# Packing the last 96 rows of an MLP weight for four token chunks into three passes of column tiles

## Chip, cores, metric

One core of a Trainium2 chip runs the whole program. The metric is the device time of one execution in microseconds (us). A kernel is run several times; executions of one kernel mostly agree within 0.3%.

Some words used below. TensorE runs the matmuls and the weight loads ahead of them; VectorE and GpSimd work element by element; ScalarE computes the Gelus and Exps; SyncE issues most of the data transfers (DMAs). PSUM is the memory that matmuls write: one bank holds the 512 f32 columns of one matmul here. A column tile is a matmul that uses 32 of the array's 128 columns, written 128*32 in the views. The chain is the profile's path of work and waits, followed back from the last instruction. A line ends with `[idle before <-releaser]` where the engine stood idle before it.

## The reference, cut to what matters

A normalised input feeds a local dilated attention (branch A) and a token mixer with an MLP (branch B); the output is x + A * silu(B). The change sits in the MLP of branch B:

```python
D, F, S = 512, 1376, 2048
x1 = x + hs                                        # mixer output
h2 = gelu(layernorm(x1) @ w3) @ w4                 # w3: 512 x 1376, w4: 1376 x 512
return x1 + h2
```

1376 is 10 x 128 + 96. So w3 gives ten full tiles of 128 rows and one of 96, for each of four chunks of 512 tokens.

## The kernel before

The program sets out its instructions in a fixed order on every engine. The w3 stage lies between the two halves of the attention: for each chunk c, six steps a, each with two row tiles in one PSUM tile of two banks; the last step holds the 96 rows alone.

```python
def w3_pair(c, a):
    pt = psa("w3_ps")                              # next of three PSUM tiles "s", "t", "o", two banks each
    fts = [ft for ft in (2 * a, 2 * a + 1) if ft < NF]          # NF = 11
    for ft in fts:
        fs = P if ft < NF - 1 else FL              # FL = 96
        for dt in range(ND):                       # ND = 4 contraction tiles of 128
            nc.tensor.matmul(pt[:fs, ft % 2, :], lhsT=w3_sb[:, dt, ft * P : ft * P + fs],
                             rhs=x1nT[c][:, dt, :], start=(dt == 0), stop=(dt == ND - 1))
    if len(fts) == 2:
        nc.scalar.activation(h3(c, 2 * a, 2), pt, AF.Gelu_apprx_tanh)
    else:
        nc.scalar.activation(h3(c, NF - 1, 1)[:FL, 0, :], pt[:FL, 0, :], AF.Gelu_apprx_tanh)
# w4_tile: eleven matmuls a token tile, the last with 96 of 128 contraction rows
# ... the stage:
for c in range(NCH):                               # NCH = 4
    for a in range((NF + 1) // 2):
        w3_pair(c, a)
        if c == 0 and a == 0:
            weighted(*prev)()                      # last attention product of half 0, and its copy from PSUM
            prev = None
            ln3_stats(2)                           # layer-norm statistics of chunk 2
            ln3_norm(2)                            # normalise, store to memory
            normalise_dn(0, 2)
            ln3_turn(2)                            # DMA transpose into x1nT[2]
            # ... the same for chunk 3 ...
        if c == 1 and a == 0:
            load_wo()
            load_w4()
            # ...
```

`scores` of attention half 1, which follows, used the PSUM tiles "s" and "t", and `weighted` used "o".

The softmax here doesn't subtract the row's maximum and nothing guards it: scores larger than these inputs give would overflow.

## Time and profile before

| | before |
|---|---|
| time, median of 5 runs | 206.06 us (206.0 to 206.35) |
| span of the profiled run | 204.1 us |
| TensorE busy | 195.2 us, 96% |
| w3 stage, first w3 matmul to first scores | 87.73 to 126.45, that is 38.72 us |
| spacing of 512-column matmuls in the stage | 0.216 us |

The span is what the profiler saw of one execution, from the first to the last instruction; the time of a run is about 2 us more than its span. "Busy" of TensorE counts overlapping matmuls once and says nothing about how well each fills the array. The lines themselves stand in the prediction.

### The profile page before, as it was taken

How to read it: one execution, taken by the hardware profiler on the slowest of the kernel's cores; microseconds unless marked ns; L12 is line 12 of the kernel's file. 1: busy time of each engine (PE TensorE's matmuls, PEld its weight loads, DVE VectorE, ACT ScalarE, POOL GpSimd, SP SyncE). 2: the span in 40 equal slices, each digit the busy share in tenths (PEclk: the TensorE clock that was granted, in tenths of full speed). 3: DMA queues.
4: the chain of work that ended last, by engine and by line, in shares of the span. 5: the costliest groups of instructions: out<-in, count | busy, mean ns of one | idle time of the engine just before them, and what ended most of it. 6: DMA issues, size and time to landing. Idle time of an engine off the chain costs nothing.

```text
span 204.1 us, 4800 instructions
## 1 busy us (share of the span) xinstructions
PE 195.2 (96%) x1900; PEld 94.9 (47%) x1928; DVE 135.0 (66%) x256; ACT 131.5 (64%) x157; POOL 74.5 (37%) x149
## 2 busy tenths in 40 slices
PE   7899999999999999999999999999999999999990
PEld 2585445444444444444444444444555444444440
DVE  5788897626298988856930101288577968888693
ACT  2366768657988888896556657898788877212130
POOL 5889842100023095964691000003830590700000
PEclk9999999999999999999999999999999999999997
DMA  5992264577900089495798948794220241553312
GB/s 146 356 348 80 87 139 86 85 109 112 275 34 5 14 199 140 75 254 107 181 196 184 295 148 136 109 278 156 36 51 5 56 89 26 116 165 118 117 51 77
DMA packets 33197, 26.74 MB, mean 131 GB/s; under 512 B 14600, under 2 KB 31088, under 8 KB 33176
## 3 DMA queue, kind: packets, MB, share of 16 engines
q1 hardware_dynamic: 30984, 23.22, 44.8%
q0 software_dynamic: 2048, 3.09, 8.9%
q8 instruction: 15, 0.25, 0.5%
q10 hardware_dynamic: 144, 0.13, 0.2%
q14 instruction: 6, 0.05, 0.1%
HBM read 12.40 MB, written 4.98 MB: 85 GB/s over the span
## 4 chain that ended last, share of the span: by engine, by line
PE 71%; DVE 11%; DMA 9%; issue 3%; POOL 3%; ACT 2%; SPq 0%; DVEq 0%; POOLq 0%
PE w_ps L501 19%; PE w_ps L521 10%; PE v_ps L547 8%; PE s_ps L567 7%; PE w_ps L457 6%; PE qk_ps L401 5%; PE w_ps L434 5%; PE o_ps L590 4%; PE qk_ps L419 4%; DMA den_d<-orw 3%; PE wo_ps L683 3%; DMA arena<-rden_d 2%; DVE arena L537 2%; DMA rden_d<-rb 1%; DVE arena L691 1%
## 5 line engine op out<-in xcount | busy, mean ns | idle before, releaser
L572 ACT ACTIVATE arena<-s_ps 128x960 bf16<-128x960 f32 (+1 forms) x68 | 62.7, 975 | 13.7 <-PE s_ps L567 13.7
L521 PE MATMUL w_ps<-arena 128*128 128x512 bf16 (+1 forms) x156 | 38.5, 380 | 0.6 <-issue 0.2
L506 ACT ACTIVATE arena<-w_ps 128x1024 bf16<-128x1024 f32 x20 | 20.5, 1024 | 14.5 <-PE w_ps L501 13.1
L632 POOL DMA_DIRECT2D arena<-orw x48 | 25.0, 528 | 5.8 <-DVE orw L602 5.8
L501 PEld LDWEIGHTS <-arena 128*128 128x128 bf16 (+1 forms) x176 | 17.5, 100 | 20.5 <-issue 0.4
L521 PEld LDWEIGHTS <-arena 128*128 128x128 bf16 (+1 forms) x176 | 16.5, 98 | 19.5
L693 POOL TENSOR_TENSOR arena<-arena 128x512 bf16<-128x512 bf16 x6 | 7.7, 1302 | 44.4 <-DVE arena L691 44.4
L536 ACT ACTIVATE sig<-arena 128x512 bf16<-128x512 bf16 x16 | 10.1, 631 | 21.0 <-DVE arena L527 20.9
L551 DVE CAST v_aug<-v_ps 128x512 bf16<-128x512 f32 x17 | 11.7, 690 | 15.4 <-PE v_ps L547 15.3
L602 DVE CAST orw<-o_ps 128x960 bf16<-128x960 f32 (+1 forms) x17 | 19.7, 1156 | 3.1 <-PE o_ps L590 3.0
L401 PE MATMUL qk_ps<-arena 128*128 128x512 bf16 (+1 forms) x109 | 20.4, 332 | 0.5 <-ACT arena L321 0.3
L501 PE MATMUL w_ps<-arena 128*128 128x512 bf16 (+1 forms) x86 | 19.4, 379 | 0.2
L501 PE MATMUL w_ps<-arena,arena 128*128 128x512 bf16 (+1 forms) x86 | 19.1, 379 | 0.1
L547 PE MATMUL v_ps<-wv_sb,arena 128*128 128x512 bf16 x67 | 17.5, 380 | 0.1
L567 PEld LDWEIGHTS <-arena 32*128 32x128 bf16 x544 | 10.2, 92 | 14.8 <-issue 14.7
L567 PE MATMUL s_ps<-arena 32*128 32x120 bf16 (+1 forms) x544 | 16.1, 213 | 0.1
L527 DVE TENSOR_TENSOR arena<-w_ps,arena 128x512 bf16<-128x512 f32 x16 | 11.0, 686 | 7.9 <-PE w_ps L521 7.9
L273 POOL TENSOR_SCALAR l3r<-l3m 128x1 f32<-128x1 f32 (+1 forms) x10 | 2.4, 238 | 37.6 <-DVE l3m L282 37.6
L457 PE MATMUL w_ps<-arena 128*128 128x512 bf16 x63 | 15.2, 380 | 0.1
L660 DVE TENSOR_TENSOR arena<-arena,orw 128x1440 bf16<-128x1440 bf16 (+1 forms) x2 | 1.6, 783 | 19.8 <-DMA orw<-rden_d 19.8
L434 PE MATMUL w_ps<-arena 128*128 128x512 bf16 x63 | 14.6, 379 | 0.0
L401 PEld LDWEIGHTS <-arena 128*128 128x128 bf16 x112 | 10.6, 98 | 7.9 <-DMA arena<-in_A_wqkv_dram 0.8
(99 smaller groups left out, 273.4 us busy)
## 6 DMA issues: line engine op xcount, KB each, us to landing
x1n_dram<-arena SPq DMA_DIRECT2D x5, 512.0 KB, 3.0
arena<-in_A_x_dram SPq DMA_DIRECT2D x4, 512.0 KB, 6.1
arena<-in_A_x_dram SPq DMA_DIRECT2D x6, 256.0 KB, 6.6
out_dram<-arena SPq DMA_DIRECT2D x6, 256.0 KB, 3.6
arena<-in_B_w_dram SPq DMA_DIRECT2D x1, 1376.0 KB
arena<-in_B_w_dram SPq DMA_DIRECT2D x1, 1280.0 KB
arena<-arena SPq DMA_DIRECT2D x16, 72.0 KB, 2.6
arena<-arena SPq DMA_DIRECT2D x16, 68.0 KB, 4.0
```

Of the source, the lines that this page charges most:

```text
L401: nc.tensor.matmul(pt[:, b, hh * w : (hh + 1) * w], lhsT=wqk_sb[:, dt, nt * P : (nt + 1) * P], rhs=xnT[p][:, dt, k * CH + hh * w : k * CH ...
L434: nc.tensor.matmul(pt[:, b, :], lhsT=w1_sb[:, dt, g * P : (g + 1) * P], rhs=xn2T[c][:, dt, :], start=(dt == 0), stop=(dt == ND - 1),)
L457: nc.tensor.matmul(pt, lhsT=w2_src(p, g, m0), rhs=w2_sb[:, g, :], start=(g == 0), stop=(g == ND - 1))
L501: nc.tensor.matmul(pt[:fs, ft % 2, :], lhsT=w3_sb[:, dt, ft * P : ft * P + fs], rhs=x1nT[c][:, dt, :], start=(dt == 0), stop=(dt == ND - 1),)
L506: nc.scalar.activation(h3(c, 2 * a, 2), pt, AF.Gelu_apprx_tanh)
L521: nc.tensor.matmul(pt, lhsT=h3(c, ft, 1)[:fs, 0, jj * P : (jj + 1) * P], rhs=w4_sb[:fs, ft, :], start=(ft == 0), stop=(ft == NF - 1),)
L547: nc.tensor.matmul(vp[:nk, :], lhsT=xnT[p][:, dt, k0 : k0 + nk], rhs=wv_sb[:, dt, :], start=(dt == 0), stop=(dt == ND - 1),)
L551: nc.vector.tensor_copy(out=va[:nk, :, 0:DH], in_=vp[:nk, :].rearrange("p (h d) -> p h d", d=DH))
L567: nc.tensor.matmul(st[:nk, b, i * nq : (i + 1) * nq], lhsT=kT[e][r : r + 32, dt, k0 : k0 + nk], rhs=qT[e][r : r + 32, dt, q0 : q0 + nq], s ...
L572: nc.scalar.activation(prv[:nk, 2 * h : 2 * h + 2], st[:nk, :, 0 : 4 * nq], AF.Exp, scale=SCALE)
L602: nc.vector.tensor_copy(out=orw[p, r][:, :, :, q0 - ra : q0 - ra + nq], in_=op[:, :, 0 : 4 * nq].rearrange("p j (s q) -> p j s q", q=nq),)
L632: nc.gpsimd.dma_start(out=oT[p][DH * hh : DH * (hh + 1), :, ra : ra + rw], in_=orw[p, r][32 * cg : 32 * cg + DH, jj],)
```

## The change

The intent: 96 rows are three column strips of 32. Four chunks have twelve such strips, and the array has room for four at once, so three passes suffice in place of four poorly filled ones. The strips of a chunk no longer lie in order, so one strip of every chunk is zero and the w4 rows are laid out to match. All four chunks must be ready when the packed part runs; it stands at the start of chunk 3.

```diff
+        nc.sync.dma_start(out=w4_sb[FL:P, NF - 1, :], in_=B_w4[F - 32 : F, :])
+    def load_w4x():                                # the same rows moved by 32, for chunks 2 and 3
+        nc.sync.dma_start(out=w4x_sb[32:P, 0, :], in_=B_w4[(NF - 1) * P : F, :])
+        nc.sync.dma_start(out=w4x_sb[0:32, 0, :], in_=B_w4[(NF - 1) * P : (NF - 1) * P + 32, :])
...
+    def w3_packed():
+        pts = [psa("w3_ps") for _ in range(2)]     # chunk c: tile c // 2, bank c % 2
+        for c in range(NCH):
+            g = 3 - c
+            nc.vector.memset(pts[c // 2][32 * g : 32 * g + 32, c % 2, :], 0.0)
+        for n, jobs in enumerate((
+            ((0, 0), (0, 1), (0, 2), (1, 2)), ((1, 0), (1, 1), (2, 1), (2, 2)), ((2, 0), (3, 0), (3, 1), (3, 2)),
+        )):
+            for dt in range(ND):
+                for g, (c, b) in enumerate(jobs):
+                    f0 = (NF - 1) * P + 32 * b
+                    nc.tensor.matmul(
+                        pts[c // 2][32 * g : 32 * g + 32, c % 2, :], lhsT=w3_sb[:, dt, f0 : f0 + 32],
+                        rhs=x1nT[c][:, dt, :], start=(dt == 0), stop=(dt == ND - 1), tile_position=(0, 32 * g),
+                    )
+            if n == 1:
+                nc.scalar.activation(h3_odd, pts[0], AF.Gelu_apprx_tanh)
+        for c in (2, 3):
+            nc.scalar.activation(h3(c, NF - 1, 1)[:, 0, :], pts[1][:, c % 2, :], AF.Gelu_apprx_tanh)
...
-            st = pst("st"[h], "s_ps")
+            st = pst(("st", "to")[p][h], "s_ps")
-        op = pst("o", "o_ps")
+        op = pst("os"[p], "o_ps")
...
-        for a in range((NF + 1) // 2):
+        if c == 3:
+            w3_packed()
+            load_wo()
+            load_w4x()
+        for a in range(NF // 2):
...
-                weighted(*prev)()
+                out = weighted(*prev)
                 prev = None
-                ln3_stats(2)
+                ln3_stats(2, 0, 2)
+                out()
+                ln3_stats(2, 2, 4)
```

More of the change, by code (lines that the diff above doesn't have):

```diff
@@ L85, in at @@
         ar, o = (arenas[0], int(kb * KB)) if kb < 170 else (arenas[1], int((kb - 176) * KB))
-        return ar[:, o : o + n * m].rearrange("p (n m) -> p n m", n=n)
+        return ar[:, o : o + int(n * m)].rearrange("p (n m) -> p n m", n=n)
     xn = [at(8 * p, M // P, D) for p in range(2)]
@@ L109 @@
     w4_sb = at(121.5, NF, D)
+    w4x_sb = at(191, 1, D)
+    h3_odd = at(60, 2, 49.5 * KB)[:, :, 0:CH]
     wo_sb = at(62, ND, D)
@@ L496, in w3_pair @@
         pt = psa("w3_ps")
-        fts = [ft for ft in (2 * a, 2 * a + 1) if ft < NF]
-        for ft in fts:
-            fs = P if ft < NF - 1 else FL
+        for ft in (2 * a, 2 * a + 1):
             for dt in range(ND):
                 nc.tensor.matmul(
-                    pt[:fs, ft % 2, :], lhsT=w3_sb[:, dt, ft * P : ft * P + fs], rhs=x1nT[c][:, dt, :],
+                    pt[:, ft % 2, :], lhsT=w3_sb[:, dt, ft * P : (ft + 1) * P], rhs=x1nT[c][:, dt, :],
                     start=(dt == 0), stop=(dt == ND - 1),
                 )
-        if len(fts) == 2:
-            nc.scalar.activation(h3(c, 2 * a, 2), pt, AF.Gelu_apprx_tanh)
-        else:
-            nc.scalar.activation(h3(c, NF - 1, 1)[:FL, 0, :], pt[:FL, 0, :], AF.Gelu_apprx_tanh)
+        nc.scalar.activation(h3(c, 2 * a, 2), pt, AF.Gelu_apprx_tanh)
+    def w3_packed():
[17 more added lines that the diff above has]
+            nc.scalar.activation(h3(c, NF - 1, 1)[:, 0, :], pts[1][:, c % 2, :], AF.Gelu_apprx_tanh)
     def w4_tile(t):
@@ L519, in half @@
             for ft in range(lo, hi):
-                fs = P if ft < NF - 1 else FL
+                w = w4_sb[:, ft, :] if ft < NF - 1 or c < 2 else w4x_sb[:, 0, :]
                 nc.tensor.matmul(
-                    pt, lhsT=h3(c, ft, 1)[:fs, 0, jj * P : (jj + 1) * P], rhs=w4_sb[:fs, ft, :],
+                    pt, lhsT=h3(c, ft, 1)[:, 0, jj * P : (jj + 1) * P], rhs=w,
                     start=(ft == 0), stop=(ft == NF - 1),
@@ L881 @@
     for c in range(NCH):
-        for a in range((NF + 1) // 2):
+        if c == 3:
[3 more added lines that the diff above has]
+        for a in range(NF // 2):
+            if c == 3 and a == 1:
+                normalise_end(0, 1)
+                normalise_end(0, 2)
             w3_pair(c, a)
             if c == 0 and a == 0:
-                weighted(*prev)()
+                out = weighted(*prev)
                 prev = None
-                ln3_stats(2)
+                ln3_stats(2, 0, 2)
+                out()
+                ln3_stats(2, 2, 4)
                 ln3_norm(2)
@@ L898 @@
             if c == 1 and a == 0:
-                load_wo()
                 load_w4()
@@ L904 @@
                 spread(1, CUT, M)
-            if c == 2 and a == 0:
-                normalise_end(0, 1)
-                normalise_end(0, 2)
     for k in range(2):
```

## The prediction

> **What bounds the kernel now.** I first read the page: busy shares, slices and the chain that ended last.
>
> ```profile
> PE 195.2 (96%) x1900; PEld 94.9 (47%) x1928; DVE 135.0 (66%) x256; ACT 131.5 (64%) x157; POOL 74.5 (37%) x149
> ...
> PE   7899999999999999999999999999999999999990
> ...
> PE 71%; DVE 11%; DMA 9%; issue 3%; POOL 3%; ACT 2%; SPq 0%; DVEq 0%; POOLq 0%
> ```
>
> TensorE is busy in nearly every slice and holds 71% of the chain, so what the change is worth is the TensorE time that it takes away, unless a wait opens. Second I read the timeline of TensorE over the w3 stage, which is the part that is rewritten.
>
> ```profile
> 87.73 1.89 PE L501 MATMUL w_ps<-arena 128*128 128x512 bf16 x8
> 89.55 0.60 PE L590 MATMUL o_ps<-arena,v_aug 128*32 128x120 bf16 x32
> 90.08 7.94 PE L501 MATMUL w_ps<-arena 128*128 128x512 bf16 x35
> 97.86 19.16 PE L501 MATMUL w_ps<-arena,arena 128*128 128x512 bf16 x86
> 116.85 9.66 PE L501 MATMUL w_ps<-arena 128*128 128x512 bf16 x43
> 126.45 0.71 PE L567 MATMUL s_ps<-arena 32*128 32x128 bf16 x16
> ```
>
> The stage runs from 87.73 to 126.45 without an idle gap. Chunk 0 holds 11 tiles of 4 matmuls. Behind the attention piece (L590), 36 matmuls remain from 90.08 to 97.86: 7.78 / 36 = 0.216 us each (a duration of 379 ns is latency; they overlap). All of chunks 1 to 3 gives 28.59 / 132 = 0.2166, which I call 0.216. Third, I read the groups by shape: does a 96-column tile cost less?
>
> ```profile
> L501 PE MATMUL w_ps<-arena,arena 128*96 128x512 bf16 x8 | 2.1, 379 | 0.0
> L501 PE MATMUL w_ps<-arena 128*96 128x512 bf16 x8 | 2.1, 379 | 0.0
> ```
>
> It does not: 379 ns, as the full ones. The last 96 rows cost 4 chunks x 4 matmuls x 0.216 = 3.45 us, with a quarter of the array empty.
>
> **What a packed pass will cost.** The kernel already has 128x32 column tiles: the attention output L590, four at a time. I looked at L590 in very narrow windows of the timeline; the first column shows when the oldest matmul still in flight had begun.
>
> ```profile
> 89.55 0.24 PE L590 MATMUL o_ps<-arena,v_aug 128*32 128x120 bf16 x4
> 89.61 0.38 PE L590 MATMUL o_ps<-arena,v_aug 128*32 128x120 bf16 x16
> 89.66 0.38 PE L590 MATMUL o_ps<-arena,v_aug 128*32 128x120 bf16 x16
> 89.71 0.38 PE L590 MATMUL o_ps<-arena,v_aug 128*32 128x120 bf16 x16
> 89.77 0.38 PE L590 MATMUL o_ps<-arena,v_aug 128*32 128x120 bf16 x16
> 89.82 0.33 PE L590 MATMUL o_ps<-arena,v_aug 128*32 128x120 bf16 x12
> 89.92 0.23 PE L590 MATMUL o_ps<-arena,v_aug 128*32 128x120 bf16 x4
> ```
>
> Four matmuls start together, and the next four 0.053 us later. At the 512-column rate that 0.216 us gives, 120 columns take 0.051 us: the four cost about what one would, and their weight loads are hidden. The price is at the ends. Chunk 0 from 87.73 to 97.86 takes 10.13 us; 44 x 0.216 = 9.50 and eight groups x 0.053 = 0.42 leave 0.21 us. I take 0.2 us for entering and leaving the tiled mode once.
>
> **What the Trainium skill says.** "TensorEngine Tiling (Array Packing)", Key Properties, says that tiles work in parallel and that changing the tiling mode drains the engine; the trace agrees, with 0.2 us for both ends. "TensorE: Matmul & The Clock Gate", Measured speedup vs the span model, gives a pack of n tiles the duration of one matmul plus about 4 ns per further tile; its 3-tile pack with 512 columns gained 2.38x. The trace of before is kinder in a stream (0.053 us per four), because one pack follows another. "PSUM — Partial Sum Buffer", The four PSUM rules, says that a group's first matmul clears status bits only in the bank and the 32-partition quadrants that it writes. So four groups can be open in four quadrants, and the zeroed quadrant survives. No run so far shows this; a correct result would.
>
> **The change, part by part.**
> (1) Removed: 16 matmuls with 96 columns, 3.45 us, all on the path.
> (2) Added: 3 passes x 4 contraction tiles = 12 groups of four, 12 x 0.216 = 2.59 us, plus one switch of mode, 0.2 us. Sum of (1) and (2): 3.45 - 2.79 = 0.66 us saved.
> (3) w4 keeps 176 matmuls, 16 of them with contraction 128 in place of 96. The groups by shape give 381 against 380 ns: nothing. The extra w4 rows are 32 + 128 rows of 1 KB, small beside the 1280 KB load.
> (4) ScalarE: four 96x512 Gelus of 0.58 us become one of 1.02 and two of 0.58. Nothing on the path, except at the end of the stage, where the last Gelu now has 1024 columns: 0.44 us later, ahead of the Exp table load (1.28) and the first two Exps (1.94).
> (5) Four 32-partition memsets on VectorE, which does little from 105 to 126; I estimate 0.6 us each from the 0.67 to 0.69 us of its other 512-element f32 work. In the built program the first packed weight load waits for those of the first tile, and a later one for those of the second. The first slot's previous Gelu ends some 2 us before the packed part, the second's some 0.5 us before. The second pair ends about 0.8 us after the packed part has begun, and is wanted at about 0.96 us, when the second pass begins. It just fits.
> (6) PSUM names of the last attention phase are rotated by one. The sequence with 24 instead of 27 allocations ends one further round, so this keeps the old distance between users. One gain: the first scores waited for a slot,
>
> ```profile
> 126.51 0.65 PE s_ps L567 x16
> 127.16 3.78 PE w_ps L521 x17
> 130.94 0.35 PE s_ps L567 x16
> ```
>
> 0.65 us where the next sixteen take 0.35. Their second slot is now released by the last but one pair's Gelu, so 0.3 us is won. But the Exps come 0.44 us later relative to TensorE, and the second scores' second half then waits for them about 0.2 us. I count 0.05 us saved net.
> (7) Statistics in two parts. Chunks now take 40 instead of 44 matmuls, so chunk 2 starts at 87.73 + 10.13 - 0.86 + 8.63 = 105.63 instead of 107.4, and chunk 3's data are wanted in the third pass at about 116.0 instead of 116.85. When do the transposed inputs come?
>
> ```profile
> 94.97 1.05 POOL L274 TENSOR_TENSOR l3r<-l3r,nhalf 128x4 f32<-128x4 f32 x1
> ...
> 101.23 2.20 SPq L488 DMA_TRANSPOSE arena<-x1n_dram  x1
> ...
> 108.55 3.21 SPq L488 DMA_TRANSPOSE arena<-x1n_dram  x1
> ```
>
> These transposes land 4.4 to 5.2 us after issue: 105.6 to 106.4 for chunk 2, just too late for 105.63. The split moves two of the four statistics into VectorE's idle time before 90.2 (1.7 us), and two normalisations ahead of the second root on GpSimd (another 0.7). The chain then ends some 2.4 us earlier, chunk 2 lands near 103.5, with 2 us in hand, and chunk 3 near 111. So this part pays nothing by itself; it protects the 0.66.
> (8) The wo load moves behind the sixteen copies of SyncE (121.5 to 132.2 before). w4 goes some 2.5 us earlier without wo and the copies follow, so wo should be issued near 128.5 and land by 135; its first matmul comes at 138.3.
>
> Sum: 0.66 + 0.05 = 0.7 us saved, 206.06 - 0.7 = 205.35 us. After the stage the path is TensorE to 172, then TensorE beside the last normalisation, all timed from TensorE, so the gain should arrive at the end undiminished.
>
> **Rivals.**
> A. The inputs are late: the packed part pulls the demand forward, and transposes and their stores vary with DMA load. If the split does not help, chunk 2 waits up to 0.8 us: 205.35 + 0.8 = 206.15, no gain. Against it are 2 us of margin.
> B. Four streams of 512 columns from four different sources do not run together. Wholly serial they would cost 48 x 0.216 = 10.4 us, so 213.8; partly, with 10% more per group, 0.26 us, so 205.6. L590 speaks against it, with four different moving operands too, but at 120 columns, in one bank.
> C. The wait moves: to memsets or, behind the stage, to the longer last Gelu or a late wo. The first costs up to 0.3 us (205.65), the second up to 0.3, a late wo perhaps 1 to 2 (206.4 to 207.4). For it speaks that (5) and (6) have margins under 0.2 us; against it that wo has 3 us.
>
> **Range and chances.** All the likely terms are tenths: 0.66 plus or minus 0.2 for group and switch, minus 0.3 for C, and run-to-run scatter of 0.15. Low end 204.9 (a switch cheaper and the score gain whole), high end 206.0 (A or two small waits). Two per cent is 4.1 us; nothing here could save it, as the whole removed work is 3.45. Slower by 4.1 needs B in full. Faster 0.01, within 2% 0.98, slower 0.01.
>
> **What would show it.** In the changed profile: packed groups of four spaced 0.216 us, the packed part near 2.8 us, the w3 stage 38.72 - 0.66 = 38.06 us from its first matmul to the first scores, no gap at the starts of chunk 2 and of the third pass, transposes of chunk 2 issued near 98.8, wo landed before its first matmul, the first scores 0.35 us. Group spacing over 0.25 us, a TensorE gap before chunk 2, or an idle TensorE before the wo matmul would make the prediction wrong.

## The result

The changed kernel took 205.22 us (median of 5, 204.95 to 205.27) against 206.06. The ratio is 0.9952, with a 95% interval of 0.9939 to 0.9966. Ratios here are the mean time of one kernel's runs over that of the other's of the same rounds, so not quite the ratio of the medians. Executions over 1.5% slower than the fastest of the same kernel are left out of the means. The forecast was 205.35, in a range of 204.9 to 206.0.

Two lines of the changed kernel's page: busy times, and the chain that ended last by engine.

```profile
PE 193.4 (95%) x1932; PEld 93.7 (46%) x1960; DVE 137.3 (67%) x260; ACT 131.6 (65%) x156; POOL 76.3 (38%) x151
...
PE 83%; DVE 7%; POOL 3%; issue 2%; ACT 2%; DMA 1%; POOLq 0%
```

TensorE sets the time, as before. The 71% of the chain that the prediction quotes is not a mark of the old kernel: a second profile of it has the chain line above word for word, 83%. Now the timeline of TensorE over the stage (start, duration, line, operation, destination and sources, count):

```profile
87.96 1.89 PE L506 MATMUL w_ps<-arena 128*128 128x512 bf16 x8
...
97.22 17.43 PE L506 MATMUL w_ps<-arena,arena 128*128 128x512 bf16 x78
114.58 0.40 PE L523 MATMUL w_ps<-arena 128*32 128x512 bf16 x3
...
116.97 0.39 PE L523 MATMUL w_ps<-arena 128*32 128x512 bf16 x3
117.29 8.81 PE L506 MATMUL w_ps<-arena 128*128 128x512 bf16 x39
126.03 0.42 PE L589 MATMUL s_ps<-arena 32*128 32x128 bf16 x16
```

The stage runs from 87.96 to 126.03: 38.07 us, 0.65 less than before. Further profiles agree: 38.08 us twice for this kernel, 38.71 for the kernel before. The packed part (L523) starts its first group at 114.58 and its twelfth at 116.97, so eleven steps take 2.39 us: 0.217 each. The last full matmul ahead of it started at 114.28 and the first full one behind it at 117.29; 3.01 us less thirteen steps of 0.216 leaves 0.20 us for both switches of mode. Nothing waits at 97.22, nor where chunk 2 starts inside that stretch.

Behind the stage, the chain in order of time shows the first two groups of scores:

```profile
126.10 0.35 PE s_ps L589 x16
...
130.23 0.63 PE s_ps L589 x16
```

The first group fell from 0.65 to 0.35 us and the second rose from 0.35 to 0.63, as forecast. From the first scores to the values behind the second it is now 4.76 us against 4.78. The next unit's first scores fell from 0.40 to 0.34.

The queue of SyncE shows when the transpose of chunk 2 and the load of wo were issued:

```profile
99.30 1.89 SPq L495 DMA_TRANSPOSE arena<-x1n_dram  x1
...
129.49 0.53 SPq L692 DMA_DIRECT2D arena<-in_A_wo_dram  x1
```

wo landed 4.2 us after its issue, at 133.7; its first matmul started at 138.44.

Where did the time go in sum? From the start of the stage to the start of the last wo matmuls it was 197.22 - 87.73 = 109.49 us before and 196.72 - 87.96 = 108.76 after: 0.73 less, of which 0.65 is the stage and 0.08 the scores (0.02 + 0.06). The last VectorE instruction follows those matmuls by 3.39 us in both. Behind it the span goes on for 3.45 us before and 3.24 after, another 0.21 us. That is no scatter: this stretch took 3.44 to 3.46 us in all three profiles of kernels without the packing and 3.22 to 3.24 in all eleven with it. It holds the end of the program, where SyncE works through a row of semaphore instructions. The view by source line shows them, before and then after (count, shortest/median/longest ns, first and last start):

```profile
L972 SPq EVENT_SEMAPHORE  x8: 17/28/28, 202.9 to 204.0; - x8
```

```profile
L999 SPq EVENT_SEMAPHORE  x5: 17/28/28, 202.3 to 203.3; - x5
```

Most start about 0.06 us apart, so three fewer account for some 0.2 us. All profiles without the packing have eight and all with it five; the change adds and moves DMAs, but why the program then needs fewer is not shown. The prediction didn't have this term. The first instructions of the stage came 0.23 us later in the changed kernel's profile; the program is the same up to there.

### The profile page after: what moved, and what is told of

Same layout as the page of the kernel before. It is cut to its first block, busy times and chain, and to the rows that moved or that the text cites. A ratio compares the mean times of both kernels' runs of the same rounds, so it can differ in the third digit from the quotient of the medians.

```text
span 203.3 us, 4876 instructions
## 1 busy us (share of the span) xinstructions
PE 193.4 (95%) x1932; PEld 93.7 (46%) x1960; DVE 137.3 (67%) x260; ACT 131.6 (65%) x156; POOL 76.3 (38%) x151
## 4 chain that ended last, share of the span: by engine, by line
PE 83%; DVE 7%; POOL 3%; issue 2%; ACT 2%; DMA 1%; POOLq 0%
PE w_ps L543 19%; PE w_ps L506 17%; PE v_ps L569 8%; PE s_ps L589 7%; PE w_ps L464 6%; PE wo_ps L705 6%; PE qk_ps L408 5%; PE w_ps L441 5%; PE o_ps L612 4%; PE qk_ps L426 4%; PE w_ps L523 1%; DVE arena L392 1%; DVE l1s L288 1%; DMA arena<-in_A_x_dram 1%; ACT arena L594 1%
## 5 line engine op out<-in xcount | busy, mean ns | idle before, releaser
L543 PE MATMUL w_ps<-arena 128*128 128x512 bf16 x155 | 38.9, 380 | 0.6 <-issue 0.2
L543 PEld LDWEIGHTS <-arena 128*128 128x128 bf16 x176 | 16.4, 98 | 19.6
L506 PEld LDWEIGHTS <-arena 128*128 128x128 bf16 x160 | 15.5, 98 | 19.2 <-issue 0.8
L506 PE MATMUL w_ps<-arena 128*128 128x512 bf16 x78 | 17.7, 379 | 0.2
L506 PE MATMUL w_ps<-arena,arena 128*128 128x512 bf16 x78 | 17.3, 379 | 0.1
L280 POOL TENSOR_SCALAR l3r<-l3m 128x1 f32<-128x1 f32 (+2 forms) x11 | 2.6, 234 | 34.3 <-DVE l3m L289 34.2
L464 PE MATMUL w_ps<-arena 128*128 128x512 bf16 x63 | 15.2, 380 | 0.1
L441 PE MATMUL w_ps<-arena 128*128 128x512 bf16 x63 | 14.6, 379 | 0.0
L408 PEld LDWEIGHTS <-arena 128*128 128x128 bf16 x112 | 10.7, 98 | 7.8 <-issue 0.4
L415 ACT CAST arena<-qk_ps 128x1024 bf16<-128x1024 f32 x11 | 11.1, 1017 | 4.5 <-PE qk_ps L408 4.5
```

Source lines behind the costliest of these rows:

```text
L408: nc.tensor.matmul(pt[:, b, hh * w : (hh + 1) * w], lhsT=wqk_sb[:, dt, nt * P : (nt + 1) * P], rhs=xnT[p][:, dt, k * CH + hh * w : k * CH ...
L441: nc.tensor.matmul(pt[:, b, :], lhsT=w1_sb[:, dt, g * P : (g + 1) * P], rhs=xn2T[c][:, dt, :], start=(dt == 0), stop=(dt == ND - 1),)
L464: nc.tensor.matmul(pt, lhsT=w2_src(p, g, m0), rhs=w2_sb[:, g, :], start=(g == 0), stop=(g == ND - 1))
L506: nc.tensor.matmul(pt[:, ft % 2, :], lhsT=w3_sb[:, dt, ft * P : (ft + 1) * P], rhs=x1nT[c][:, dt, :], start=(dt == 0), stop=(dt == ND - 1),)
L543: nc.tensor.matmul(pt, lhsT=h3(c, ft, 1)[:, 0, jj * P : (jj + 1) * P], rhs=w, start=(ft == 0), stop=(ft == NF - 1),)
```

## The experiments

My theory was that the gain is TensorE time alone, 12 groups of four at the price of 12 matmuls instead of 16, less one switch of mode, and that the split statistics and the rotated PSUM names only keep waits from opening. The rivals were that the split itself pays, that groups cost by their tiles, that the switch is free, and that the boundary behind the stage hides a cost. The kernel before had medians of 206.03 to 206.07 us, in 9 to 11 runs.

### The split alone

```diff
 # the kernel before
-                weighted(*prev)()
+                out = weighted(*prev)
                 prev = None
-                ln3_stats(2)
+                ln3_stats(2, 0, 2)
+                out()
+                ln3_stats(2, 2, 4)
```

> The kernel before with chunk 2's statistics in two parts and nothing else. Theory (the gain is TensorE time of the packed passes, the split only makes data arrive earlier): the transpose of chunk 2 is issued some 2.4 us earlier (near 98.8 instead of 101.2 us), TensorE does not notice, and the time stays at 206.06 within 0.15. Rival (the split itself shortens the path): 205.4 or less.

Measured: 206.2 us, ratio 1.0005 (0.9991 to 1.0018). The transpose of chunk 2 was issued at 98.94 instead of 101.23, and the stage took 38.71 us. The split moves the issue 2.3 us forward, and by itself pays nothing.

### The packing without the split

```diff
 # the changed kernel
-                ln3_stats(2, 0, 2)
                 out()
-                ln3_stats(2, 2, 4)
+                ln3_stats(2)
```

> The changed kernel with chunk 2's statistics in one part again. Theory: the transpose of chunk 2 is issued near 101.4 us and lands 4.4 to 5.2 us later, at 105.8 to 106.6, while TensorE wants it at 105.85; so a TensorE gap of 0 to 0.8 us opens at the start of chunk 2, and the time is 205.2 to 206.0, most likely 205.6. Rival (data of chunk 2 had slack anyway, the split is idle): 205.2 with no gap.

Measured: 206.71 us (206.49 to 207.06), ratio 1.0035: slower than before the change. The chain in order of time, for the kernel without the split:

```profile
101.31 5.89 DMA arena<-x1n_dram
107.20 0.05 issue
107.24 8.81 PE w_ps L506 x40
```

The transpose landed at 107.20. TensorE had started chunk 1 at 97.11 and was through it 40 x 0.216 = 8.64 us later, so chunk 2 started 1.5 us late. The stage took 39.57 us, again 1.5 more than the changed kernel's, and the time rose by 206.71 - 205.22 = 1.49. So the mechanism was right and its size was not: I had expected 0 to 0.8 us, from landings 4.4 to 5.2 us after the issue, and this one took 5.9. Was that scatter?

> A second profile of the changed kernel with undivided statistics. If the late transpose of chunk 2 (landed 5.9 us after its issue) is how this kernel always runs, the gap before chunk 2 is again 1.3 to 1.6 us and the time 206.5 to 207.0. If it was scatter between executions, the gap is nearer to the 0 to 0.8 us first expected.

Measured: 206.76 us; issue at 101.37, landing 5.95 us later, TensorE idle for 1.40 us. It is how this kernel runs: all five timed runs above took at least 206.49 us.

> A second profile of the kernel before. If its transpose of chunk 2, issued near 101.2 us, also moves data only from about 105.6 us on, then the slow start belongs to this place in the program, and the kernel before hid it because it wanted chunk 2 only at 107.4 us; if the data move from 103.6 us on again, the slow start belongs to the kernel without the split.

Measured: 206.11 us; issue at 101.39. The throughput of the DMA engines in slices of 0.2 us shows the plateau of about 290 GB/s, which I take to be the transpose's data, from about 104.2 us on, and from 103.6 in the first profile of the kernel before. In the two profiles with the packing but without the split it begins only at about 105.6 and 106.0, after slices of at most about 50 GB/s. So the slow start goes with the kernel without the split. The two kernels are the same up to there but for the matmuls of the chunks and their Gelus, and the plateau begins about when TensorE runs out of chunk 1. I can't say that one causes the other; this stays open.

### The old PSUM names

```diff
 # the changed kernel
-            st = pst(("st", "to")[p][h], "s_ps")
+            st = pst("st"[h], "s_ps")
-        op = pst("os"[p], "o_ps")
+        op = pst("o", "o_ps")
```

> The changed kernel with the PSUM names of the last attention phase as before. Theory: the first scores now ask for the slot of the very last Gelu, which ends about 1.2 us after the last w3 matmul, so TensorE stalls there about 1.2 us, the table load and Exps come no earlier, and the time is 206.0 to 206.6. Rival (the rotation is cosmetic, slots are free anyway): 205.2.

Measured: 206.19 us, median of three runs, ratio 1.0006; a fourth run was slow (209.99) and is left out. The timeline of TensorE at the first scores:

```profile
127.07 0.43 PE L589 MATMUL s_ps<-arena 32*128 32x128 bf16 x16 [1.11 <-ACT arena L510]
```

TensorE waited 1.11 us for the last Gelu, which held the tile "s". Without these two changed lines, the whole gain would have gone into that wait.

### Three tiles in a pass instead of four

```diff
 # the changed kernel; w4 rows in plain order for all chunks, the zero strip is the fourth
-            ((0, 0), (0, 1), (0, 2), (1, 2)), ((1, 0), (1, 1), (2, 1), (2, 2)), ((2, 0), (3, 0), (3, 1), (3, 2)),
+            ((0, 0), (0, 1), (0, 2)), ((1, 0), (1, 1), (1, 2)), ((2, 0), (2, 1), (2, 2)), ((3, 0), (3, 1), (3, 2)),
```

> The changed kernel with three column tiles in a pass, one chunk a pass, so four passes in place of three. Theory (a group costs what one stream of 512 columns costs, 0.216 us, however many tiles it has): 16 groups instead of 12, the packed part 3.55 to 3.65 us instead of 2.71, the w3 stage 38.93 us, and the time 0.86 above the changed kernel: 206.1, that is the time before or a shade more, since the mode switch (0.2) stays. Rival (a group's cost is by tiles, 4 x 0.054): the packed part stays at 2.7 us and the time at 205.2.

Measured: 206.14 us (206.04 to 206.16). The packed part in the chain:

```profile
114.69 3.56 PE w_ps L523 x48
```

The same 48 matmuls in 16 groups take 3.56 us; in 12 groups the chain gave them 2.70. Each group costs 0.86 / 4 = 0.215 us, however many tiles it has. The stage was 39.09 us, 0.16 more than expected. The waits name it: a weight load of L506 waited 0.5 us for the transposed input at the start of chunk 1, and chunk 1 began at 97.24 where the 32 matmuls from 90.19 on would have ended at 97.10. In this run the data of chunk 1 came too late by about 0.15 us.

### The price of a switch of mode

```diff
 # the changed kernel; dummies(k) issues k full 128x512 matmuls into a spare PSUM tile
+        dummies(8)                                 # first kernel: all in front of the packed part
...
+            if n < 2:
+                dummies(4)                         # second kernel, instead: after passes 1 and 2
```

> The changed kernel with eight full 128x512 matmuls of no use in front of the packed part. Theory: 8 x 0.216 = 1.73 us more in the stage and no further switch of mode; from the first dummy to the first full matmul behind the packed part 1.73 + 2.7 + 0.1 = 4.5 us; time 206.9.

> The same eight dummies, four after the first packed pass and four after the second, so the tiled mode is entered and left three times instead of once. Theory (each entry and exit costs 0.2 us): 0.4 us more than with the dummies in front, stage and time alike, 207.3. Rival (the switch is free when the queue is full, and the 0.2 us belonged to something else): the same time as with the dummies in front, 206.9.

Measured: 206.97 us with the dummies in front, 207.38 with the dummies between. The first scores in the timeline of TensorE, dummies in front, whose stage began at 87.92:

```profile
127.72 0.42 PE L598 MATMUL s_ps<-arena 32*128 32x128 bf16 x16
```

And with the dummies between, whose stage began at 87.38:

```profile
127.62 0.42 PE L598 MATMUL s_ps<-arena 32*128 32x128 bf16 x16
```

That is 39.80 and 40.24 us. The eight dummies cost 39.80 - 38.07 = 1.73 us, and the two additional rounds through the tiled mode 0.44 us, 0.22 each. The switch is real. The stages are compared here and not the times, because the profiled run with the dummies between was the lowest of its four (206.95; the others 207.35 to 207.45): its stage began half a us early. A wait of 0.27 us for GpSimd ahead of the matmuls of L382, at 36.8 us in the changed kernel's second profile, is absent in it; the rest of the half is not traced.

### Can the boundary be improved?

The second scores wait for Exps that the last, 1024-column Gelu holds up. So I cut that Gelu in two.

```diff
 # the changed kernel, in w3_pair, after the four matmuls of row tile ft
+            if c == 3 and a == NF // 2 - 1:
+                nc.scalar.activation(h3(c, ft, 1)[:, 0, :], pt[:, ft % 2, :], AF.Gelu_apprx_tanh)
```

> The changed kernel with the last Gelu of the w3 stage cut into two of 512 columns, the first of which can start while the second tile is still computed. Theory (the longer last Gelu delays the table load and the first Exps, and the second scores wait for these): ScalarE reaches the Exps about 0.4 us earlier, the second scores take 0.35 to 0.4 us instead of 0.63, and the time falls by 0.25 to 0.3 us, to about 204.95. Rival (the second scores wait for something else, or the gain is lost again in the next unit): 205.2.

> The changed kernel once more, so that the next run can be set beside it on the same chip: 205.2 within 0.15, second scores of the first unit of the last phase held up about 0.3 us (16 matmuls in 0.6 to 0.7 us).

Measured: 206.09 us with the halved Gelu, 205.05 for the changed kernel again (204.64 to 205.25). The halved Gelu lost 1 us. The timeline of TensorE shows why:

```profile
125.86 1.02 PE L506 MATMUL w_ps<-arena 128*128 128x512 bf16 x4 [0.74 <-ACT arena L511]
```

The last four matmuls waited for the first half's Gelu (L511). They write the other bank, but of the same PSUM tile, and the trace names ScalarE as what they waited for. So I gave the two row tiles a PSUM tile of one bank each.

```diff
-        pt = psa("w3_ps")
+        last = c == 3 and a == NF // 2 - 1
+        if last:
+            cnt["p"] += 1                          # keeps the later order of names
+        else:
+            pt = psa("w3_ps")
         for ft in (2 * a, 2 * a + 1):
+            po = psb("w3_ps") if last else pt[:, ft % 2, :]
             # ... four matmuls into po; if last, a Gelu from po
```

> The changed kernel with the last two w3 tiles in two PSUM tiles of one bank each instead of one tile of two banks, and a Gelu for each. In the halved-Gelu run the last four matmuls waited 0.74 us for the first half's Gelu, because both halves lay in one PSUM tile. Theory (that wait came from the shared tile, and behind it the idea holds): no wait before the last four matmuls, the Exps start about 0.4 us earlier against the first scores, the second scores take 0.35 us instead of 0.63, and the time falls 0.25 to 0.3 us below the changed kernel of the same call. Rival (the second scores wait for something else, or the next unit gives it back): the same time as the changed kernel.

> The changed kernel beside the run with two one-bank tiles: 205.1 to 205.2, second scores 0.63 us.

Measured: 205.21 us (204.74 to 205.34) against 205.15 for the changed kernel, ratios to before 0.9955 and 0.9952. The chain in order of time, with one-bank tiles:

```profile
130.11 0.35 PE s_ps L597 x16
...
153.93 0.68 PE s_ps L597 x16
```

The wait before the last matmuls is gone, and the second scores take 0.35 us, so the theory holds there: the scores at about 149 us start 149.45 - 149.13 = 0.32 us earlier than in the changed kernel's profile (0.06 of it because the stage began earlier). But the scores at 153.93 take 0.68 us where the changed kernel's took 0.41, and from there on the two run within 0.04 us of each other. In front of these scores an Exp started 0.76 us after its own scores had started (151.59 to 152.35), where 0.48 is usual in both kernels. The trace names only the scores as its releaser, and these were long done. So the gain was made and given back 22 us later, to something that I could not name. It is no accident of one profile: the kernel with the halved Gelu shows the same there, its Exp 0.77 us behind the start of its scores. It is not a better kernel by these runs; that two of its five runs were at 204.74 and 204.78 proves nothing, as the changed kernel has such runs too.

## Why the prediction was right

- **Bound.** Right: the gain is TensorE time. But the share of the chain was a poor measure of it: 71% was one profile of the kernel before, its second profile has 83%, and the split alone 84%. In the first, a normalisation's DMA of 4.63 us stood in the chain's tail; yet the last VectorE instruction came 3.39 us behind the start of the last wo matmuls, as in the others.
- **Step 1 and step 2, the packed passes.** Right: groups 0.216 us apart (forecast 0.216), both switches 0.20 (0.2), the stage 38.07 us (38.06). The tile count and the dummies tested both terms by themselves: 0.215 per group and 0.22 per switch. Rival B, that four 512-column streams would hinder each other, is out. (Its 213.8 us for a wholly serial run should read 213.1: 10.37 - 2.59 on top of 205.35; the verdict stays.) The open point on PSUM is answered too: every run of the experiments that carries the packed passes was correct, so four groups open at once and the zeroed quadrant do no harm here.
- **Step 3, w4 with 128 rows.** No run tested it alone; the sum leaves no room for a cost.
- **Step 5, memsets.** The estimate of 0.6 us each was too high; they took 0.48. They still only just fit: the last ended at 115.30, and the second pass began at 115.46. My sum had left 0.16 too, but by two errors that cancel: the memsets were shorter, and VectorE stood idle for 0.17 us between the last two, for which I had put nothing:

```profile
114.16 0.48 DVE L516 MEMSET w_ps<- 32x512 f32 x1 [0.57 <-ACT arena L510]
114.82 0.48 DVE L516 MEMSET w_ps<- 32x512 f32 x1 [0.17 <-DVE w_ps L516]
```

- **Step 6, the PSUM names and the longer Gelu.** The direction was right: first scores 0.35, second 0.63. The sum, 0.08 us for a forecast of 0.05, is partly luck: the first unit won only 0.02, because the second scores waited 0.28 us and not 0.2, and 0.06 came in the next unit, which had no forecast. The count of 24 instead of 27 names is wrong as well: the code takes 24 before and 22 after, and 22 is one more than seven rounds of three, which is why the ring must turn by one. The old names cost 1.0 us, which I had not put in numbers.
- **Step 7 and rival A, the late inputs.** The direction was right: the split pays nothing alone and protects the gain; with it, the transpose of chunk 2 was issued at 99.30 (forecast 98.8), and 98.92 and 98.94 in later profiles. The size was wrong. "If the split does not help, chunk 2 waits up to 0.8 us" failed: it waits 1.5 us, because the transpose landed 5.9 us after its issue, not 4.4 to 5.2. I had taken those landings from two other transposes of the same kernel. Nor did I look at chunk 1: shortening chunk 0 by four matmuls asks for it 0.86 us earlier too, and one run here waited 0.15 us for it.
- **Step 8, wo.** Issued at 129.49 (forecast 128.5), landed at 133.7 (by 135), wanted at 138.44. Harmless. So of rival C only the wait of the second scores came, which step 6 had counted.
- **The rest.** The steps explain 0.73 us, and the five against eight semaphore instructions at the program's end 0.21, together 0.94. The medians differ by 0.84 us in the first result and by 1.01 and 0.92 later, each more than the 0.7 forecast. That second term was in no step, so that it fell on the side of the gain is luck.

## What to carry to other kernels

When ragged row tiles of several blocks share one weight, packing them pays by the group: count groups of up to four, price each as one matmul of that length (0.216 us at 512 columns here), and add one switch of mode (0.2 us here) for each time the tiled part is entered. Work that is pulled together must have its data together: compute the new deadline of every input and measure that input's own landing, for one late transpose turned a gain of 0.84 us into a loss of 0.68 (206.71 against 206.03). Shortening a stage also changes which buffer its last user holds, so walk the ring of PSUM names through the boundary before trusting the sum. And take a second profile before reading a share of the chain as a property of the kernel.

## What the Trainium skill lacked or had wrong

- "TensorEngine Tiling (Array Packing)", Key Properties: says that a switch of mode drains the engine, without a figure. Here one round into 128x32 tiles and out cost 0.20 us, and two more rounds 0.44 us.
- "TensorE: Matmul & The Clock Gate", Measured speedup vs the span model: prices one pack by itself, with about 4 ns for each further tile. In a stream of packs four tiles cost no more than one full matmul: groups of four and of three both took 0.215 to 0.217 us at 512 columns, a full matmul 0.216.
- The same page, Back-to-back issue gap: gives about 131 ns for each 512-column matmul in a stream with weight loads, and says that 216 ns over-counts. Here a stream of weight load and matmul pairs ran at 216 ns in every kernel (7.78 us for 36).
- "DMA: Bandwidth & Descriptors", Latency and other measured facts: gives a bandwidth for DMA transposes, but no time from issue to landing. Here 512 tokens by 512 landed after 4.4 to 7.6 us, 5.9 and 5.95 where the split was missing, and what delays the slow ones is open.
- No page that I read says that cutting a reader of a two-bank PSUM tile in two makes the writer of the other bank wait, where dependences are kept by tile: 0.74 us here.
